# A new written-out order for attention and expert layers on one core, with its opening and its end listed word by word

## The chip, the cores and the metric

The kernel runs on one core of a Trainium2 chip. The metric is the device time of a whole execution in microseconds (us); the kernel before takes 478.36 us (median of three runs, 478.16 to 478.54). A profile of one execution has, for each engine, the start and length of every instruction, and for each DMA queue the packets that it moved. The engines are TensorE (PE, matmuls into PSUM), VectorE (DVE), ScalarE (ACT), GpSimd (POOL, which here issues the loads that change the type) and SyncE (SP, which issues stores and transposing DMAs).

## The reference

Linformer attention, then a two-layer network with a sigmoid-weighted activation:

```python
k_proj = np.einsum('ks,bhsd->bhkd', E, k)
v_proj = np.einsum('ks,bhsd->bhkd', F, v)
scores = scale * np.matmul(q, k_proj.transpose(0, 1, 3, 2))
attn = np.exp(scores - max);  attn = attn / sum(attn)
x = attn @ v_proj                      # (batch, seq, heads * 64)
h = x @ w_in;  g = h / (1 + np.exp(-1.702 * h))
out = g @ w_out
```

There are 8 batches of 8 heads, 1024 positions and 64 numbers a head, 64 projected keys, and layers of 512 x 2048 and 2048 x 512. Inputs and output are float32.

## The kernel before, in words

The 8192 tokens are cut into 16 blocks of 512, so two blocks (j = 2b and 2b + 1) make a batch b. For a batch, k and v are loaded (`load_kv`, one DMA each, into the single buffers `k_sb` and `v_sb`), projected by 16 matmuls with 64 columns of weights (`proj`, line 183), and k is transposed on its way by a DMA on SP (`kts`). q is loaded in eight DMAs (`load_q`, line 70) and transposed by SP (`q_dma`, line 263) into `qT`. For a block, the scores (`sc`, line 273) come out of `eight`: eight matmuls on tiles of 64 x 32 that run side by side. ACT takes the exponential (`ex`), TensorE sums it (`su`, line 719) and multiplies it with v (`va`, line 273), and DVE scales the result with the reciprocal sums (`mv`, line 713). Those sums travel from PSUM through `den`, a gathering DMA (`ga`), a reciprocal on DVE (`rc`), a write to memory (`sr`) and a spreading read into `rbc` (`sb`), the DMAs all on SP. Blocks 1 and 2 instead do it with tokens on the partitions (`tok`, `x_tr`).

Layer 1 of blocks 0, 1 and 2 is done plainly, 64 matmuls of 512 columns (`ffn1`, line 426), and so is layer 2 of block 0 (`ffn2`, line 438). All else uses seven half-size products instead of eight (the scheme of Strassen and Winograd): a layer is split into quarters, so that 112 matmuls of 256 columns do the work of 64 of 512. Layer 1 is cut into four groups u0 to u3 with products `P1` to `P7` (line 677), layer 2 into `F1` to `F7`, two parts each (line 637, or 533 where `ffn2_parts` makes them). Between products, partial sums are copied (`c1`, `c2`, `c3`, `Fc1` to `Fc3`, line 620 and 681) and added (`d1`, `d2`, `Fd1`, `Fd2`, line 623), and the activation (`g11` to `g22`, line 693) reads the sums. `x_sum` and `g_sum` prepare the differences of the inputs, `w_sums` and `w_in_sums` those of the weights, once; the four w_in differences lie in `late`.

The order of work is written by hand. Blocks 0 to 2 come from loops with a table of extra work (`at`, `filled`). From block 2's second layer on, a list of words, `STEPS`, is read once per block: `u1.P5+1` is product 5 of group 1 of the next block, `sc.0+3` the scores of the block three ahead. Each engine does its own words in the order of the list; a word waits for its inputs and for its buffer. `BANK` names the PSUM bank that each result uses, so a word also waits until the bank's last reader is done. `AHEAD` inserts words the first time round. `pj`, `kb`, `kd`, `vq` are the projection and the copies of its result, `ld` and `lq` the loads of the next batch's k and v and of its q, `qd` q's transpose. `ld` has to wait for `pj`, which reads the same buffers, and a load of q for the transpose that reads the q tile before it in the same buffer:

```python
return ldpool.tile([P, J, H, D], BF16, name="q_even" if b in (0, 2) else "q_sb")
```

`q_even` is later reused for `uu`, the partial sums of the u groups, and in block 2 for a temporary of `w_in_sums`. A word `hold` makes POOL wait for a transposed k before it issues the loads behind it.

Of the kernel before, what the change touches and what calls it, by code (L numbers as in the profile page):

```python
# [17 lines left out]
def kernel(ctx, tc, q, k, v, E, F,  # L18
                                                     moe_w_in, moe_w_out, out):
    nc = tc.nc  # L20
# [41 lines left out]
    def q_buf(b):  # L62
        return ldpool.tile([P, J, H, D], BF16, name="q_even" if b in (0, 2) else "q_sb")

    def load_q(b, j0=0):
        if j0 == 0:
            qt[b] = q_buf(b)
        qv = q[b].rearrange("h (p j) d -> p j h d", p=P)
        for j in range(j0, J):
            nc.gpsimd.dma_start(out=qt[b][:, j], in_=qv[:, j])  # L70

    def load(b):
        for what in ("kvq", "kqv", "kvq", "qkv")[min(b, 4) - 1]:
            if what == "q":
                load_q(b)
            elif what == "k":
                load_kv(k, kt, b, "k_sb")
            else:
                load_kv(v, vt, b, "v_sb")
# [19 lines left out]
    for i in range(8):  # L99
        if i == 7:  # L100
            load_q(0, JB)
        load_w_in(i)
    for i in range(4):
        sl = slice(i * FC // 4, (i + 1) * FC // 4)
        nc.gpsimd.dma_start(out=w_out_sb[:, sl, :], in_=w_out_v[:, sl, :])
    load(1)


# [110 lines left out]
    def v_out(b, v_ps):  # L219
        vv = v_ps[HI].rearrange("k (u x) d -> k u x d", x=4)  # L220
        for r, xs_ in ((LO, X_LO), (HI, X_HI)):
            if b == 1:
                vx = vx1[r, :, :D].rearrange("k (u x) d -> k u x d", x=4)
                nc.vector.tensor_copy(vx[:, :, xs_], vv[:, :, xs_])
            nc.vector.tensor_copy(vqs[b % 2][r].rearrange("k (u e) d -> k u e d", e=2), vv[:, :, xs_, :])

    def kv_out(b, cp=nc.vector.tensor_copy):
        def go():
            ps = kvps.pop(b)
            k_b = att.tile([KP, H, D], BF16, name="k_b")  # L230
# [45 lines left out]
    def x_tile():  # L276
        return x_any([P, TB])

    def scores(h, u, half=None, x=False):
        b, c = divmod(h, NB2)  # L280
        j0, n = (c * JB, JB) if half is None else (c * JB + half * JB // 2, JB // 2)
        ts = slice(j0 * P - c * TB, (j0 + n) * P - c * TB)

        def go():
            if h not in expT:
                expT[h] = att.tile([P, HP, TB], BF16, name="expT", bufs=3)
            s_ps = [(x_tile() if x else f_tile([P, TB]))[:, :n * P] for _ in range(2)]
            eight(s_ps, [kts[b % 2][:, 2 * u + i, :] for i in range(2)],
                 [q0s[half][u][:, :, i, :] if h == 0 else qT[b][:, j0:j0 + n, 2 * u + i, :]
                   for i in range(2)], KP if h == 0 else 32)  # L290
            for i in range(2):
                nc.scalar.activation(expT[h][:, 2 * u + i, ts], s_ps[i], AF.Exp, scale=scale)
        return go
# [9 lines left out]
    def sums(h):  # L303


        def go():
            d_ps = [x_any([P, TB]), bank(5, [P, TB])]
            for p in range(HP):
                for e in range(2):
                    r = HI if (p + e) % 2 else LO  # L310
                    nc.tensor.matmul(d_ps[e][32 * p:32 * p + 32], ones[r, :32], expT[h][r, p, :], start=True, stop=True)
            den = att.tile([P, 2, TB], F32, name="den", bufs=1)
            for e in range(2):
                nc.vector.tensor_copy(den[:, e, :], d_ps[e])
            rdens[h] = den
        return go

# [7 lines left out]

    def spread(h, q=nc.sync, recip=True):
        def go():
            rc = rdens.pop(h)
            n = rc.shape[1]
            if recip:  # L330
                nc.vector.reciprocal(rc, rc)
            rdr = dram.tile([HP, 2, TB], F32, name="rdr")
            q.dma_start(out=rdr.rearrange("p e (r n) -> (p e r) n", n=n), in_=rc)
            rbc[h] = att.tile([P, HP, TB], F32, name="rbc", bufs=1)
            for e, r in enumerate((LO, HI)):
                q.dma_start(out=rbc[h][r], in_=rdr[None, :, e, :].to_broadcast([D, HP, TB]))
        return go

    def norm(h, u):
        def go():  # L340
            e = [expT[h][:, 2 * u + i, :] for i in range(2)]
            d_ps = [x_any([P, TB]) for _ in range(2)]
            eight(d_ps, [ones, ones], e)
            n_ps = [x_any([P, TB]) for _ in range(2)]
            eight(n_ps, [vqs[h // NB2 % 2][:, 2 * u + i, :] for i in range(2)], e)
            for i in range(2):
                rd = att.tile([P, TB], F32, name="rdn")
# [82 lines left out]
    def ffn2(j, n, fcs):  # L430
# [4 lines left out]
        if fcs.start == 0:  # L435
            o_ps[n] = f_tile([P, DM])
# [499 lines left out]
```

The softmax here doesn't subtract the row's maximum and nothing guards it: scores larger than these inputs give would overflow.

## Time and profile before

| what | value |
|---|---|
| median of three runs | 478.36 us |
| profiled execution: span from first to last instruction | 474.7 us |
| what lies outside the span, by the median | 3.7 us |
| TensorE busy (its ends are modelled) | 463.9 us, 98% |
| DVE, ACT, POOL busy | 316.6, 322.1, 83.2 us |
| matmuls of layer 1 and 2 in seven products | lines 677, 637 and 533 |
| small-tile matmuls (scores, values, sums) | 240, 208 and 96 + 8 in groups of eight |
| packets of POOL's queue, of SP's | 86816 (30.43 MB), 46020 (37.84 MB) |
| TensorE clock granted | full |

A row of a timeline is: start, length, engine, line, operation, what is written from what, how many, and in brackets how long the engine stood idle before it and what released it. The lengths of matmuls overlap, so the distance between starts tells their cost. The profile gives no time of its own for the profiled execution beyond its span.

### The profile page before, as it was taken

How to read it: one execution, taken by the hardware profiler on the slowest of the kernel's cores; microseconds unless marked ns; L12 is line 12 of the kernel's file. 1: busy time of each engine (PE TensorE's matmuls, PEld its weight loads, DVE VectorE, ACT ScalarE, POOL GpSimd, SP SyncE). 2: the span in 40 equal slices, each digit the busy share in tenths (PEclk: the TensorE clock that was granted, in tenths of full speed). 3: DMA queues.
4: the chain of work that ended last, by engine and by line, in shares of the span. 5: the costliest groups of instructions: out<-in, count | busy, mean ns of one | idle time of the engine just before them, and what ended most of it. 6: DMA issues, size and time to landing. Idle time of an engine off the chain costs nothing.

```text
span 474.7 us, 10486 instructions
## 1 busy us (share of the span) xinstructions
PE 463.9 (98%) x4323; PEld 356.2 (75%) x4331; DVE 316.6 (67%) x587; ACT 322.1 (68%) x559; POOL 83.2 (18%) x104
## 2 busy tenths in 40 slices
PE   8999999998999999999999999999999999999997
PEld 4644447556778788887878788787888878888885
DVE  4503895498486776858686685868667685958562
ACT  2665456566696777868686786957687786758472
POOL 7562161061051200501050010500000000000000
PEclk9999999999999999999999999999999999999999
DMA  9999999989799999937999299942371403602022
GB/s 169 200 188 207 228 192 152 232 169 180 114 212 207 200 200 238 110 92 162 211 216 130 94 152 214 172 95 97 90 182 38 121 25 91 177 5 90 0 90 90
DMA packets 132964, 69.19 MB, mean 146 GB/s; under 512 B 98341, under 2 KB 122421, under 8 KB 132917
## 3 DMA queue, kind: packets, MB, share of 16 engines
q0 software_dynamic: 86816, 30.43, 57.5%
q1 hardware_dynamic: 46020, 37.84, 32.8%
q8 instruction: 34, 0.56, 0.5%
q10 hardware_dynamic: 80, 0.26, 0.2%
q14 instruction: 14, 0.11, 0.1%
HBM read 72.88 MB, written 16.99 MB: 189 GB/s over the span
## 4 chain that ended last, share of the span: by engine, by line
PE 91%; DMA 3%; ACT 3%; DVE 2%; POOL 1%; issue 1%; DVEq 0%; ACTq 0%; POOLq 0%
PE k_ps L677 34%; PE k_ps L637 33%; PE k_ps L426 9%; PE k_ps L533 5%; PE k_ps L273 3%; PE k_ps L438 3%; PE k_ps L183 3%; DMA v_sb<-in_v_dram 3%; ACT gT L693 1%; PE k_ps L719 1%; DVE xT L713 1%; POOL k_sb L58 0%; POOL v_sb L58 0%; PE k_ps L398 0%; PE k_ps L413 0%
## 5 line engine op out<-in xcount | busy, mean ns | idle before, releaser
L623 DVE TENSOR_TENSOR q_even<-k_ps,q_even 128x512 f32<-128x512 f32 x104 | 70.5, 689 | 54.4 <-PE k_ps L677 53.2
L677 PE MATMUL k_ps<-xw,late 128*128 128x256 bf16 x624 | 89.5, 273 | 0.6 <-DVE xw L499 0.6
L677 PEld LDWEIGHTS <-late 128*128 128x128 bf16 x832 | 80.4, 98 | 12.8 <-PE k_ps L637 2.3
L637 PEld LDWEIGHTS <-sg 128*128 128x128 bf16 x832 | 81.2, 98 | 10.7 <-issue 1.4
L693 ACT ACTIVATE gT<-k_ps 128x512 bf16<-128x512 f32 x104 | 62.3, 601 | 25.3 <-PE k_ps L677 23.7
L637 PE MATMUL k_ps<-tw,sg 128*128 128x256 bf16 x624 | 76.8, 273 | 0.3 <-DVE u_sb L620 0.3
L677 PEld LDWEIGHTS <-w_in_sb 128*128 128x128 bf16 x624 | 58.2, 98 | 18.1 <-issue 11.3
L637 PEld LDWEIGHTS <-gT 128*128 128x128 bf16 x624 | 61.0, 98 | 7.8 <-issue 0.4
L620 ACT COPY q_even<-k_ps 128x512 f32<-128x512 f32 x65 | 37.0, 591 | 42.8 <-PE k_ps L677 42.0
L677 PE MATMUL k_ps<-xT,w_in_sb 128*128 128x256 bf16 x416 | 62.2, 273 | 1.0 <-ACT vq L620 1.0
L693 ACT ACTIVATE gT<-q_even 128x512 bf16<-128x512 f32 x104 | 61.4, 631 | 0.0
L70 POOL DMA_DIRECT2D q_sb<-in_q_dram x48 | 42.1, 904 | 106.5 <-DMA qT<-q_sb 70.1
L637 PE MATMUL k_ps<-w_out_sb,gT 128*128 128x256 bf16 x416 | 51.6, 273 | 0.1
L426 PE MATMUL k_ps<-xT,w_in_sb 128*128 128x512 bf16 (+1 forms) x195 | 42.4, 370 | 0.3
L507 DVE TENSOR_TENSOR sg<-gT 128x1024 bf16<-128x1024 bf16 (+2 forms) x64 | 41.4, 649 | 1.6 <-ACT gT L693 1.5
L428 ACT ACTIVATE gT<-k_ps 128x512 bf16<-128x512 f32 (+1 forms) x50 | 28.9, 580 | 18.0 <-PE k_ps L426 17.7
L426 PEld LDWEIGHTS <-w_in_sb 128*128 128x128 bf16 x200 | 19.3, 98 | 21.3 <-issue 0.8
L713 DVE TENSOR_TENSOR xT<-k_ps,rbc 128x512 bf16<-128x512 f32 x52 | 33.5, 680 | 0.0
L677 PE MATMUL k_ps<-xw,w_in_sb 128*128 128x256 bf16 x208 | 31.3, 273 | 0.0
L677 PE MATMUL k_ps<-xT,late 128*128 128x256 bf16 x208 | 31.2, 273 | 0.0
L681 ACT COPY k_ps<-k_ps 128x512 f32<-128x512 f32 x52 | 29.2, 588 | 2.7 <-DVE xT L713 1.2
L620 DVE COPY q_even<-k_ps 128x512 f32<-128x512 f32 x39 | 25.7, 686 | 8.0 <-PE k_ps L677 8.0
(136 smaller groups left out, 561.2 us busy)
## 6 DMA issues: line engine op xcount, KB each, us to landing
out_dram<-o_sb SPq DMA_DIRECT2D x31, 512.0 KB
rbc<-rdr SPq DMA_DIRECT2D x24, 512.0 KB
k_sb<-in_k_dram POOLq DMA_DIRECT2D x7, 1024.0 KB, 10.2
v_sb<-in_v_dram POOLq DMA_DIRECT2D x7, 1024.0 KB, 15.2
q_sb<-in_q_dram POOLq DMA_DIRECT2D x48, 128.0 KB, 6.4
w_in_sb<-in_moe_w_in_dram POOLq DMA_DIRECT2D x8, 256.0 KB, 10.8
w_out_sb<-in_moe_w_out_dram POOLq DMA_DIRECT2D x4, 512.0 KB, 11.5
q_even<-in_q_dram POOLq DMA_DIRECT2D x12, 128.0 KB, 13.2
```

The lines of the kernel that those rows point to most:

```text
L70: nc.gpsimd.dma_start(out=qt[b][:, j], in_=qv[:, j])
L426: nc.tensor.matmul(h_ps, w_in_sb[:, kc, fc * P:(fc + 1) * P], xT[j][:, kc, ts], start=(kc == 0), stop=(kc == KC - 1))
L428: nc.scalar.activation(gts[j][:, fc, ts], h_ps, AF.Gelu_apprx_sigmoid)
L507: nc.vector.tensor_tensor(t[i - 1], in0, in1, op=ALU.add if i == 1 else ALU.subtract)
L533: nc.tensor.matmul(dst, a[:, k, tc_ * P:(tc_ + 1) * P], w[:, k], start=(first and (one or tc_ == 0) and k == 0), stop=(final and k == FH - 1),
L620: (nc.scalar.copy if n in ON_ACT else nc.vector.tensor_copy)(out_, in_)
L623: nc.vector.tensor_tensor(out_, in0, in1, op=ALU.add)
L637: nc.tensor.matmul(live[n][:, t], x[:, c, t * P:(t + 1) * P], w[:, c], start=(i in (1, 5) and t == 0 and c == 0), stop=(i in (2, 3, 4) and ...
L677: nc.tensor.matmul(live[h][:, r], a[:, c, f:f + P], w[:, c], start=(i in (1, 5) and r == 0 and c == 0), stop=(i in (2, 3, 4) and r == 1 an ...
L681: nc.scalar.copy(new(f"B{m}", [P, 2, TH]), live[f"A{m}"])
L693: nc.scalar.activation(out_, in_, AF.Gelu_apprx_sigmoid)
L713: nc.vector.tensor_tensor(x_of(j)[:, u, :], live[f"V{p[1]}{t}"], rbc[j][:, u, :], op=ALU.mult)
```

## The change

The steady list is replaced by one that needs two stretches of small tiles in a block: the projection with both score groups between `F1.0` and `F1.1`, and values, sums, values at the end. It is used for nine blocks (j = 4 to 12). What comes before and after it is written out in two further lists, `OPEN` and `TAIL`, in which `@` gives the block, `:` the PSUM banks and `/A` or `/D` the engine of a copy. Block 0's first layer stays a loop. In `OPEN`, `O` is block 0's second layer, `L` and `Lg` block 1's first layer and its activation, `tk`, `tr`, `tm`, `xt`, `xc` the token-wise attention of blocks 1 and 2, `ws` and `wi` single weight sums, `s0` the stores of block 0, `qda` and `qdb` the two halves of batch 1's q transpose. Block 2's first layer now goes through the u groups, so that `uu` takes `q_even` there, the temporary of `w_in_sums` moves into `sg`, and only batch 0's q is kept in `q_even`. Most weight sums of layer 1 are made while block 0's first layer runs. The last piece of w_in is loaded ahead of the second half of batch 0's q, batch 1's q is loaded in two halves with v between, and `hold` is gone. More banks are named, and copies move between DVE and ACT.

```diff
     def q_buf(b):
-        return ldpool.tile([P, J, H, D], BF16, name="q_even" if b in (0, 2) else "q_sb")
-
-    def load_q(b, j0=0):
+        return ldpool.tile([P, J, H, D], BF16, name="q_sb" if b else "q_even")
+
+    def load_q(b, j0=0, j1=J):
         if j0 == 0:
             qt[b] = q_buf(b)
         qv = q[b].rearrange("h (p j) d -> p j h d", p=P)
-        for j in range(j0, J):
+        for j in range(j0, j1):
             nc.gpsimd.dma_start(out=qt[b][:, j], in_=qv[:, j])
...
     nc.gpsimd.dma_start(out=q0_sb, in_=q[0].rearrange("h (p j) d -> p h j d", p=P)[:, :, :JB])
     load_kv(v, vt, 0, "v_sb", 2)
     for i in range(8):
-        if i == 7:
-            load_q(0, JB)
         load_w_in(i)
+    load_q(0, JB)
     for i in range(4):
         sl = slice(i * FC // 4, (i + 1) * FC // 4)
         nc.gpsimd.dma_start(out=w_out_sb[:, sl, :], in_=w_out_v[:, sl, :])
-    load(1)
+    load_kv(k, kt, 1, "k_sb")
+    load_q(1, 0, JB)
+    load_kv(v, vt, 1, "v_sb")
+    load_q(1, JB)
...
+    def w_in_sums(i, copy=nc.vector.tensor_copy, cols=slice(None)):
+        tmp = sg[:, 2:].rearrange("p i c t -> p (i c t)").bitcast(F32).rearrange("p (c f) -> p c f", c=KC // 2)
+        if i == 5:
+            return copy(late[:, 1], tmp)
+        out_, in0, in1, op = ((late[:, 0], a21, a22, ALU.add), (late[:, 2], a11, a21, ALU.subtract),
+                              (tmp, a21, a22, ALU.add), (tmp, tmp, a11, ALU.subtract),
+                              (late[:, 3], a12, tmp, ALU.subtract))[i]
+        nc.vector.tensor_tensor(out_[..., cols], in0[..., cols], in1[..., cols], op=op)
...
+    OPEN = """
+        sc.1@1:7,4 qda@2 sc.0@1:5,6 O.1.0@0:0 O.1.1@0 O.3.0@0:2 ex.0.0@1 tk.0.0@1:5 tr.0.0@1 ex.0.1@1 ex.1.0@1
+        tm.0.0@1 O.2.0@0:3 ex.1.1@1 O.3.1@0 tk.0.1@1:5 O.1.2@0 tk.1.1@1:7 tr.0.1@1 tm.0.1@1 tk.1.0@1:5 O.1.3@0
...
+        L.9@1:6 Lg.2@1 ws.1@1 vq.1@2/A vx.0@2 Lg.15@1 ld@2 L.11@1:4 gs1.1@1 Lg.0@1 Lg.11@1 F1.0@1:3 kd@2 Lg.9@1
+        s0.0@0 s0.1@0 qdb@2 sc.0@2:0,2 sc.1@3:5,6 gs3.1@1 ws.3@1 gs3.0@1 ex.0.0@2 sc.0@3:1,4 gs1.0@1 ex.0.1@3
...
+        ex.0.0@3 ex.0.1@2 ex.1.0@3 F1.1@1 tk.0.0@2:7 pj@4:0 Fc1@1:1/A gs2.0@1 ws.5@1/D gs2.1@1 kb@4/D tr.0.0@2
+        sc.1@2:4,2 tk.0.1@2:5 F6.0@1 tr.0.1@2 vq.0@4/A ex.1.0@2 tk.1.0@2:4 lq@2 kd@4 tm.0.1@2 tm.0.0@2 ex.1.1@2
+        tr.1.0@2 F6.1@1 tk.1.1@2:7 F2.0@1 vq.1@4/D gt@5 tm.1.0@2 tk.2.0@2:2 tr.1.1@2 xt.0@2:4 F5.0@1:5 qd@4
...
+        sc.0@4:7,1 u1.P7@2 ex.0.1@4 ex.0.0@4 u0.d2@2 Fd2@1 rc@3 ld@4 sc.1@4:0,5 ex.1.0@4 ex.1.1@4 u0.P7@2
+        u0.P2@2 u3.P1@2:7 su@4:5,1 xs.3@2 u1.d1@2 u0.d1@2 den.0@4/D den.1@4/D u0.g11@2 u1.P4@2 u1.g21@2 u0.g22@2
...
     STEPS = """
-        F3.0-1 u2.c1 Fo1-1 u0.d2 rc+2 F3.1-1 u2.P5 u3.c3 u3.P7 u0.g22 Fd2-1 u2.P6 u0.g12 u2.c2 u2.c3 u2.P2
-        u2.g11 u3.P3 va.0+1 u3.d1 st0-1 gs1.0 u3.P2 u3.d2 u3.g11 u2.P3 u3.g12 mv.0.1+1 u2.P7 va.1+1 pj+4 ld+4
-        u3.g22 u3.P4 u2.d2 st1-1 u2.g12 u3.g21 u2.d1 mv.0.0+1 kb+4 F1.0 mv.1.0+1 u2.g22 vq.0+4 u2.P4 mv.1.1+1
-        gs1.1 u2.g21 vq.1+4 F1.1 u0.P1+1 sr+2 sc.0+3 gs2.0 gs2.1 sc.1+3 Fc1 ex.0.0+3 gs3.0 u1.P1+1 xs.0+1
-        ex.1.1+3 xs.2+1 gs3.1 F2.0 F2.1 ex.1.0+3 xs.1+1 kd+4 ex.0.1+3 F6.0 F6.1 Fc2 u0.c1+1 su+3 u1.c1+1 gt+1
-        u0.P6+1 den.0+3 u0.P2+1 Fo0 den.1+3 gs4.1 u1.P6+1 F7.0 u1.P2+1 u1.P5+1 u0.c2+1 F5.0 u1.c2+1 u0.g11+1
-        u1.c3+1 F5.1 ga+3 Fc3 u1.P7+1 F7.1 u1.g11+1 xs.3+1 gs4.0 u1.P3+1 u2.P1+1 u0.P5+1 u1.d1+1 u3.P1+1 Fd1
-        u0.c3+1 u1.P4+1 F4.0 u0.P7+1 sb+2 u1.d2+1 u0.d1+1 qd+4 lq+4 u1.g21+1 u3.c1+1 F4.1 u1.g12+1 u3.P6+1
-        u3.c2+1 u0.P4+1 u1.g22+1 u3.P5+1 u0.P3+1 u0.g21+1
+        F1.0 pj+4 mv.1.1+1 u3.g22 mv.0.0+1 u2.g12 mv.1.0+1 xs.0+1 sc.1+3 gs2.0 ga+2 sc.0+3 kb+4 F1.1 vq.0+4
+        u1.P1+1 vq.1+4 gs1.1 xs.1+1 gs2.1 Fc1 kd+4 ex.1.1+3 u1.P5+1 F2.1 ex.1.0+3 u1.c3+1 F2.0 rc+2 Fo0 xs.3+1
+        ld+4 F6.0 u1.c1+1 gs3.1 lq+3 F5.0 u0.P5+1 gs4.1 F6.1 u1.P6+1 st1-1 ex.0.0+3 ex.0.1+3 gt+4 sr+2 u0.P1+1
+        u0.c1+1 xs.2+1 F5.1 u1.P3+1 qd+4 gs3.0 Fc2 u0.c3+1 u0.P2+1 u1.c2+1 u1.d2+1 gs4.0 F7.0 u1.P2+1 u0.g11+1
+        u2.P1+1 u2.c1+1 F7.1 Fc3 u0.P3+1 u2.P2+1 Fd1 u0.P6+1 u1.P7+1 u1.g11+1 u1.d1+1 sb+2 u0.c2+1 F4.1 u3.P1+1
+        u0.d2+1 F4.0 u1.P4+1 Fo1 u0.g12+1 u1.g21+1 u0.P7+1 u1.g22+1 u3.c1+1 F3.1 u1.g12+1 u2.g11+1 u3.P5+1
+        u2.P6+1 F3.0 u0.d1+1 u2.P5+1 u0.g22+1 u3.c3+1 u3.P6+1 u2.c2+1 u2.c3+1 u2.P7+1 u3.P3+1 gs1.0+1 u3.c2+1
+        u3.P2+1 Fd2 u3.P7+1 u0.P4+1 u2.d1+1 u2.g22+1 u2.P4+1 u3.g11+1 u0.g21+1 u3.d1+1 u2.P3+1 u3.P4+1 va.0+2
+        u2.g21+1 u3.d2+1 u2.d2+1 mv.0.1+2 st0 su+3 u3.g21+1 va.1+2 den.0+3 den.1+3 u3.g12+1
     """.split()
-    BANK = dict(FD=0, FB=4, FG=0, A0=6, A1=1, B0=7, B1=3, G0=2, G1=5, S10=5, S11=7, V00=4, V01=0,
-                S00=3, S01=2, V10=6, V11=5, D0=2, D1=5, PJ=1)
-    ON_ACT = ('Fc1', 'Fc3', 'c2.2', 'c3.0', 'c3.1', 'c3.2', 'c3.3', 'vq')
-
-    held = consts.tile([1, 1], BF16, name="held")
...
+        u3.P3@15 u3.P2@15 u2.P7@15 F3.0@14 u2.P3@15 F3.1@14 u3.d2@15 u2.d1@15 u2.d2@15 u3.g22@15 u3.g11@15
+        u3.g12@15 u1.g21@15 u2.g22@15 u2.g12@15 Fd2@14 gs1.0@15 u3.P4@15 F1.0@15:7 u2.P4@15 F1.1@15 gs1.1@15
+        f5.1@15:0 gs2.0@15 gs2.1@15 gs4.0@15 gs3.1@15 u2.g21@15 Fc1@15:5/A F6.0@15 F6.1@15 Fc2@15/A fc3.1@15
+        u3.g21@15 f5.0@15:2 st0@14 st1@14 F7.0@15 F7.1@15 gs4.1@15 fc3.0@15 f3.0@15 Fd1@15 F4.1@15 F4.0@15
+        F2.0@15 F2.1@15 Fo1@15/A fd2.0@15 f3.1@15 fd2.1@15 st2.0@15 st1@15 Fo0@15/A st0h@15 st2.1@15
+    """.split()
+    BANK = {"D0":1, "D1":5, "FB":1, "FD":3, "FG":0, "PJ":1, "S00":5, "S01":7, "S10":4, "S11":0, "V00":6, "V01":0,
+            "V10":2, "V11":7, "u0.A":7, "u0.B":5, "u0.G":3, "u1.A":6, "u1.B":4, "u1.G":2, "u2.A":7, "u2.B":2,
+            "u2.G":3, "u3.A":6, "u3.B":4, "u3.G":1}
+    ON_ACT = ("Fc1", "Fc2", "den.0", "den.1", "kb", "u0.c1", "u0.c2", "u0.c3", "u1.c1", "u2.c1", "u2.c3", "u3.c2",
+              "vq.0", "vq.1")
...
+        on_act = (name in ON_ACT) if eng is None else eng == "A"
+        copy = nc.scalar.copy if on_act else nc.vector.tensor_copy
...
+        elif i == "O":
+            n, g = int(p[1]), t
+            if g == 0:
+                new(f"O{n}", [P, DM])
+            for fc in range(4 * g, 4 * g + 4):
+                nc.tensor.matmul(live[f"O{n}", j], gts[j][:, fc, n * P:(n + 1) * P], w_out_sb[:, fc, :],
+                                 start=(fc == 0), stop=(fc == FC - 1))
+        elif i == "L":
+            gts[j] = gT
+            h_ps = new(name, [P, TB])
+            for kc in range(KC):
+                nc.tensor.matmul(h_ps, w_in_sb[:, kc, t * P:(t + 1) * P], xT[j][:, kc, :],
+                                 start=(kc == 0), stop=(kc == KC - 1))
+        elif i == "Lg":
...
         elif i == "pj":
-            kvps[b] = new("PJ", [P, H, D])
-            proj(b)()
-        elif i == "hold":
-            nc.gpsimd.tensor_copy(held, kts[b % 2][:1, 0, :1])
-        elif i == "ld" and b + 1 < B:
+            kv_ps = new("PJ", [P, H, D])
+            for n in range(J):
+                for e, r in enumerate((LO, HI)):
+                    nc.tensor.matmul(kv_ps[r], eft(n, slice(e * KP, (e + 1) * KP)), (kt, vt)[e][b][:, :, n, :],
+                                     start=(n == 0), stop=(n == J - 1))
+        elif i == "ld":
             load_kv(k, kt, b + 1, "k_sb")
...
+            else:
+                nc.vector.tensor_copy(vx1[r, :, :D].rearrange("k (u x) d -> k u x d", x=4)[:, :, xs_], vv)
+        elif i in ("qd", "qda", "qdb"):
+            q_dma(b, *{"qd": (0, J), "qda": (0, JB), "qdb": (JB, JB)}[i])()
+        elif i == "lq":
             load_q(b + 1)
-        elif i not in ("ld", "lq"):
+        else:
             raise KeyError(name)
 
...
-    AHEAD = {
-        (2, None):
-            "F1.0@2 F1.1@2 Fc1@2 sc.1@4 sc.0@4 ex.1.0@4 ex.1.1@4 F2.0@2 ex.0.0@4 ex.0.1@4 F2.1@2 sc.1@5 "
-            "F6.0@2 sc.0@5 F6.1@2 ex.1.0@5 ex.1.1@5 ex.0.0@5 ex.0.1@5 gt@3 Fo0@2 Fc2@2 va.0@3:6,1 va.1@3:5,7 "
-            "mv.0.0@3 mv.0.1@3 mv.1.0@3 mv.1.1@3 F7.0@2 su@4:0,3 den.0@4 den.1@4 ga@4 ",
-        (2, "u1.c1+1"): "F7.1@2",
-        (2, "u2.P1+1"): "rc@4 sr@4 sb@4 qd@6 pj@6:1 kb@6 kd@6 vq.0@6 vq.1@6 hold@6 ld@6 lq@6",
-    }
-
...
+    first = [(half, fc) for half in range(2) for fc in range(2)] + [(None, fc) for fc in range(2, FC)]
+    for i, (half, fc) in enumerate(first):
+        ffn1(0, fc, slice(0, TB) if half is None else slice(half * TB // 2, (half + 1) * TB // 2))
+        if i == 12:
+            for cols in (slice(0, DH // 2), slice(DH // 2, DH)):
+                w_in_sums(2, cols=cols)
+            w_in_sums(3)
+            w_in_sums(0)
+        if i in (15, 16):
+            q_tr(i - 13)()
+    w_in_sums(1)
+
+    BATCH = ("qd", "pj", "kb", "kd", "vq", "ld", "lq")
+
+    def due(name, j):
+        kind = name.split(".")[0]
+        if kind in BATCH and j % NB2:
+            return False
+        return j < (NBLK - NB2 if kind in ("ld", "lq") else NBLK)
+
+    def listed(words):
+        for word in words:
             name, n = word.split("@")
+            n, _, eng = n.partition("/")
             n, _, banks = n.partition(":")
-            step(name, int(n), [int(x) for x in banks.split(",")] if banks else None)
-            done.add((name, int(n)))
-
-    done = set()
-    for j in range(2, NBLK):
-        last = j == NBLK - 1
...
+    listed(OPEN)
+    for j in range(4, NBLK - 3):
         for word in STEPS:
-            m = word.replace("-", "+-").split("+")
-            name, n = m[0], j + int(m[1] if len(m) > 1 else 0)
-            if last and name[0] in "Fs" and n == j and name[:2] not in ("sc", "su", "sr", "sb"):
-                if name[1:2].isdigit() and name[0] == "F":
-                    parts.pop(tail.pop(0))()
-            elif due(name, n, j) and (name, n) not in done:
-                step(name, n)
-            ahead(j, word)
-    for f in parts.values():
-        f()
-    assert not fill, fill
+            name, _, n = word.replace("-", "+-").partition("+")
+            if due(name, j + int(n or 0)):
+                step(name, j + int(n or 0))
+    listed(TAIL)
```

## The prediction

> **What bounds the kernel now.** First the page's head and its chain of waits:
>
> ```profile
> span 474.7 us, 10486 instructions
> PE 463.9 (98%) x4323; PEld 356.2 (75%) x4331; DVE 316.6 (67%) x587; ACT 322.1 (68%) x559; POOL 83.2 (18%) x104
> PE 91%; DMA 3%; ACT 3%; DVE 2%; POOL 1%; issue 1%; DVEq 0%; ACTq 0%; POOLq 0%
> ```
>
> TensorE sets the end; DVE and ACT have a third to spare. So the change is worth what it takes out of TensorE's stream, less what makes TensorE wait. Then the timeline of TensorE in a steady block (start, length, count) and around two waits:
>
> ```profile
> 275.35 0.60 PE L677 MATMUL k_ps<-xT,w_in_sb 128*128 128x256 bf16 x4
> 275.88 0.62 PE L273 MATMUL k_ps<-qT,kt 64*32 64x512 bf16 x16
> 276.43 0.61 PE L677 MATMUL k_ps<-xT,w_in_sb 128*128 128x256 bf16 x4
> 276.88 1.91 PE L637 MATMUL k_ps<-w_out_sb,gT 128*128 128x256 bf16 x16
> ...
> 115.14 0.61 PE L677 MATMUL k_ps<-xw,late 128*128 128x256 bf16 x4 [0.59 <-DVE xw L499]
> ...
> 123.99 0.60 PE L677 MATMUL k_ps<-xT,w_in_sb 128*128 128x256 bf16 x4 [1.04 <-ACT vq L620]
> ...
> 460.35 1.03 PE L533 MATMUL k_ps<-w_out_sb,gT 128*128 128x256 bf16 x8 [0.86 <-ACT k_ps L564]
> ```
>
> Starts, not the modelled lengths, give the pitch: 276.88 to 278.63 is 16 matmuls of 256 columns, 0.109 each. A 128x512 one takes 0.216 (56 between 89.90 and 101.99, the next row's start). 275.35 to 276.43 is 1.08 for four products (0.44) and two groups of eight small tiles (0.216 each): 0.21 is left over. The same sum for a lone group of eight (`su` at 280.47) leaves 0.22. So a visit to small tiles costs 0.22, however many groups it holds. Row by row, TensorE makes 57 visits after 36.49, four in a block.
>
> Third, the queues that feed TensorE. POOL's timeline, which issues the loads, and SP's, which issues stores and transposes (start, length of the issue):
>
> ```profile
> 60.38 0.87 POOL L58 DMA_DIRECT2D k_sb<-in_k_dram  x1 [4.47 <-PE k_ps L183]
> 299.23 7.00 POOL L70 DMA_DIRECT2D q_sb<-in_q_dram  x8 [24.41 <-DMA qT<-q_sb]
> ...
> 64.15 5.73 SPq L263 DMA_TRANSPOSE qT<-q_sb  x1
> 81.91 7.16 SPq L263 DMA_TRANSPOSE qT<-q_even  x1
> ```
>
> The first is k2, released by the projection that freed `k_sb`; the second a q load that stood 24.41 until the transpose of the q before it had left `q_sb`. Last, the packets that POOL's queue (q0) and SP's (q1) moved in the microseconds from 67, from 83 and from 88 (count, MB):
>
> ```profile
> q0 software_dynamic: 156, 0.16, 93.6%
> q1 hardware_dynamic: 157, 0.04, 30.4%
> ...
> q0 software_dynamic: 204, 0.21, 125.0%
> ...
> q1 hardware_dynamic: 1131, 0.29, 127.7%
> ```
>
> POOL's k load alone moves 204 packets a us (1 KB each), SP's transpose alone 1131 (256 B). Together they move 156 and 157: one for one, so the transpose falls to a seventh of its speed. I take 157 for each when both have work.
>
> [...] I use 1 us, since POOL wakes at 299.2 when the transpose's packets have ended some 2 us before, and at 188.9 some 1 us after them. [...]
>
> **The change part by part**, in us, against the profiled execution (474.7; its start and end outside the span are 3.7 against the median 478.36).
>
> Block 2, layer 1: 64 x 0.216 = 13.83 becomes 112 x 0.109 = 12.22: -1.6. The zeros matmul goes: -0.2.
>
> Visits: in the new lists I count 32 after the opening instead of 57: 25 x 0.22 = -5.5.
>
> Waits in the old order that go with it: the larger gaps above the pitch, 1.2 at 123.99, 1.0 at 460.35, 0.8 at 115.14, six of 0.35 to 0.6 between 73 and 111: some -5.0. Waits that the new order brings: F2.1 needs Fc1, with only one product (0.44) between, where the copy and the end of the matmul take about 0.55: 0.1 in each of ten blocks; sc.1@1 now comes straight after the q_tr copy (36.52): 0.15; the tail about 0.5; DVE's rc@3 below 0.3: +2.0, with 0.5 to 6 as bounds.
>
> Costed at nothing: ON_ACT moves copies between ACT (0.59) and DVE (0.69); of 26.9 a block I add ACT 17.7 and DVE 19.7. Tight spots of a block (u.P4 after d1, u.P6 after c1, mv after va) keep 0.1 to 0.8. Four repeated table words and the reloads around split exponentials (1.28 each, perhaps 10 in all) lie in an opening where ACT has 78 of 118; without cover, each would cost up to 1.28. The w_in sums (2.29, 2.29, 1.19, 1.19) go to DVE while it idles 12.6 before q_tr's copy at 34.52. They need w_in's last piece, which now precedes q's second half, so the packet counts put it at 27.8, and they end at 32.5; without that slack q_tr is late by the difference. w_out's sums and the k and v evictions lie beside 512-column products as before. On POOL w_in's last piece moves ahead of q's second half, which lands about 1.3 later (near 31.7; q_tr wants it at 33.9), and v1 moves behind half of q1.
>
> Now the queues. Of the q tiles only batch 0's keeps `q_even` (which becomes `uu` in block 2), so batch 2's q (q2) goes into `q_sb`, which q1 holds until its second transpose, qdb@2, has landed. Before, q2 was loaded at 61.24 without it. And ld@2 issues k2 and v2 (2048 packets) together; before, v2 went out at 74.47.
>
> First wait. PE reaches pj@2 at 36.49 + 19.5 of listed work + 0.5 = 56.5, v1 lands about 56 (its 1024 packets follow q1's first half; `qda` shares the end). It ends at 58.4; k2/v2 issue 58.8, full rate 3.2 later at 62. SP: kd@2 behind kb@2 (59.4), two stores of block 0 (from 60.7), qdb@2 at about 62.3, when q1's last packets have landed. The stores' 256 packets of 4 KB share with k2: 3.8, to 66.3. Then qdb's 2048 packets against the 1650 left of k2/v2: 1650/157 = 10.5; the rest 0.4; seen at 78.2. sc.1@3 reads that half; PE is there at 36.49 + 32.7 + 1.0 = 70.2: **waits 8.0**. Behind it is all of PE; pj@4 too (v2 is in at 77.8).
>
> Second wait. lq@2 starts 78.4; eight issues and 8192 packets take 9.4 to 9.6 (299.23 to 308.8), seen 88.6. On POOL ld@4 stands right behind (its buffers are free once pj@4 ends, near 82), so k3/v3's packets follow from 88. qd@4 starts at 88.7, packets 2.7 later; k3/v3 have 1350 left: 1350/157 = 8.6, then 2746/1131 = 2.4, seen 103.4. PE, after 78.2, has 19.2 of work and 0.7 of visits: sc.0@4 at 98.1, **waits 5.3**. (Before, a copy to `held` kept POOL 20.68 at 136.06 until a kt transpose, issued behind qd@6, had landed, and only then let k4/v4 go; it is removed.) On SP, ga@3 queues behind qd@4, so rc@3 and the u1.d1 behind it on DVE come at about 105.8; u1.P4 needs it at 106.
>
> In the steady blocks with a projection the same order (sb behind qd on SP, ld beside it) puts rbc down some 3 before mv.0.1 reads it: k/v's last 1150 packets share for 7.3, the transpose's rest takes 5, rbc 2.4, from an issue 7 after the block's start to 22 to 24 of 27.7. So nothing; if that cover is gone, its lateness stands on DVE ahead of all four multiplies and xs.0, which the next block's products read.
>
> Sum: 474.7 - 1.6 - 0.2 - 5.5 - 5.0 + 2.0 + 8.0 + 5.3 = 477.7; +3.7 = **481.4**. A move within 0.2% (0.96) is about what a measurement can't tell from none.
>
> **Rivals.** (1) *Only the first wait*: k3/v3 don't meet qd@4. Alone it ends 8.6 after its start (81.91 to about 90.5), seen 98.3, level with PE: 472.6 + 3.7 = 476.3. For it: 85 to 91 had such a transpose to itself. Against: POOL holds nothing between lq@2 and ld@4. (2) *The other side, faster*: loads don't hold up SP's transposes. qdb is then seen at 67.8, no wait; pj@4 waits 5.7 for v2 and q2's transpose (seen 93.9) is hidden: 470.1 + 3.7 = 473.8; with no wait at all 468.1. It decides when q2's transpose is seen before 100.4: the two waits then total under 10.3, which is what the rest gains. Against it is the 157 against 157. (3) *The steady order stalls too*: 0.5 to 1.0 per block at the tight spots, nine blocks: 486 to 490. For it: slacks of 0.1. (4) The change doesn't do what it says: products or visits stay; I see both in the lists, so under 0.01.
>
> **How the numbers follow.** Likeliest 0.50: 477.5 to 486 (slower 0.44, same 0.06). Rival 1, 0.18: 474 to 478.5 (faster 0.12, same 0.06). Rival 2, 0.14, faster. Rival 3, 0.18, slower. Faster 0.26, same 0.12, slower 0.62. 473.5 to 487 leaves about one in ten on each side (the no-wait part below, the worst of rival 3 above).
>
> **What would show it.** PE's timeline should have one gap of 5 to 10 ahead of the small tiles near 70 to 78, released by the qT transpose, and one of 2 to 8 near 98 to 103; POOL's q2 load starting near 78 after `DMA qT<-q_sb`; steady pairs of blocks of about 54 instead of 54.8; 512-column matmuls of L gone from block 2. I am wrong if the transpose lands by 72, if q2's load starts before it, or if steady blocks lengthen.

## The result, and the profile after

The changed kernel takes 507.64 us (median of 5; 506.91 to 510.83) against 478.36 (5 runs, 478.11 to 478.54): 1.063 times the time before, 95% interval 1.060 to 1.066. The prediction was 481.4, at most 487: the direction is right, the size is not. (One of the five executions of `i_halves` below, at 501.68, was a slow one and is left out of that run's ratio.)

The page's head, its row of the granted TensorE clock over 40 slices of 12.7 us, and its chain (the profiled execution took 510.83; the clock row of the kernel before is 9 throughout):

```profile
span 509.1 us, 10598 instructions
PE 470.7 (92%) x4372; PEld 367.8 (72%) x4378; DVE 334.9 (66%) x603; ACT 323.2 (63%) x557; POOL 80.4 (16%) x100
PEclk9999996979979999999997999979999999999999
PE 50%; DMA 29%; SPq 9%; issue 7%; POOL 2%; DVE 1%; ACT 1%; POOLq 0%; DVEq 0%; ACTq 0%
```

TensorE was 91% of the chain and is 50%; DMA has 29% and SP's issues 9%. The clock has dips, which the kernel before has not. TensorE's timeline has these gaps (start, length, count, in brackets the idle time ahead and what ended it):

```profile
80.83 1.05 PE L249 MATMUL k_ps<-qT,kt 64*32 64x512 bf16 x16 [9.82 <-DMA qT<-q_sb]
108.93 0.63 PE L249 MATMUL k_ps<-qT,kt 64*32 64x512 bf16 x8 [5.40 <-DMA qT<-q_sb]
148.56 1.01 PE L605 MATMUL k_ps<-xT,w_in_sb 128*128 128x256 bf16 x4 [4.82 <-DVE xT L641]
...
216.43 0.41 PE L249 MATMUL k_ps<-qT,kt 64*32 64x512 bf16 x8 [2.91 <-DVE xT L641]
273.67 1.21 PE L249 MATMUL k_ps<-qT,kt 64*32 64x512 bf16 x12 [2.65 <-DVE xT L641]
335.08 1.21 PE L249 MATMUL k_ps<-qT,kt 64*32 64x512 bf16 x12 [4.13 <-DVE xT L641]
```

The first two are the waits that the prediction placed near 70 to 78 and 98 to 103, at 9.8 and 5.4 instead of 8.0 and 5.3. The other four, 14.5 in all, it did not have. They stand behind DVE's multiplies (`mv`, L641), and DVE's table of waits says what these wait for (in all, times, longest):

```profile
DVE xT L641 <- DMA rbc<-rdr: 20.8, 4, 8.0
```

That is `sb`, the spread of the reciprocals: four times, 20.8 in all. One such place on the chain, in order of time (start, length):

```profile
199.13 7.76 SPq L239
...
207.00 0.61 SPq L664
...
207.66 7.90 DMA rbc<-rdr
...
215.69 1.30 DVE xT L641 x2
```

SP is in the issue of the q transpose `qd` (L239) until 206.9; only then can `sb` (L664) go, and it lands 7.9 later. In the kernel before, the view of the tile `rbc` has for this link:

```profile
DMA to landing us min/median/max: 4.9/5.9/6.9
```

The transpose, issued at 191.3, is slow because of the loads beside it. Packets of POOL's queue (q0) and of SP's (q1) in the microsecond from 199, and of SP's from 207, when the loads had ended (count, MB, share of the 16 engines):

```profile
q0 software_dynamic: 149, 0.15, 89.4%
q1 hardware_dynamic: 150, 0.04, 29.1%
...
q1 hardware_dynamic: 1134, 0.29, 127.6%
```

The one near 148, in the opening, is of another make: `qd` takes only 4.9 there. `sb` of block 4 stands behind it on SP and goes at 137.6, and `rbc` is read at 147.8, while a load of q, issued at 137.9, moves its packets beside it (460 in the microsecond from 141).

Then the clock. Windows around the gap at 271 (from and to, length; busy time and count of PE, PEld, DVE, ACT and POOL; granted clock; DMA share; GB/s):

```profile
271.00:272.00 1.00, 0.03 (x4) 0.00 (x0) 0.00 (x0) 1.00 (x3) 1.00 (x3) 1.00 1.01 316
273.00:274.00 1.00, 0.33 (x8) 0.12 (x8) 1.00 (x2) 0.00 (x0) 1.00 (x2) 0.50 2.33 166
276.00:277.00 1.00, 1.00 (x7) 0.69 (x6) 1.00 (x3) 0.20 (x1) 0.00 (x0) 0.50 1.24 363
281.00:282.00 1.00, 1.00 (x11) 0.90 (x10) 1.00 (x3) 0.98 (x2) 0.00 (x0) 1.00 0.31 24
```

The clock falls to 0.50 about 2 after the last matmul and is back to 1.00 only near 279.8, 6.1 after TensorE resumed. The same windows behind the gaps ending at 80.8, 108.9, 148.6 and 335.1 show 4.4, 3.6, 4.9 and 6.1 of work at half clock; the gap before 216.4 has none. Four products that take 0.44 at 1.00 take 0.85 at 0.50 (starts at 276.50 and 277.35), so half of these 25.1 is lost, by estimate: 12.6. In all five stretches the whole windows read 0.50. Counted from the fall to the return, idle time included, the stretches are more regular: from 272 to 280 the windows read 0.97, six times 0.50, and 0.61, which is 0.06 + 6 + 0.78 = 6.84 at half clock. The other four come to 10.24, 6.82, 6.82 and 6.84: two or three times 3.41. The prediction had not priced any of it.

The account against the predicted span of 477.7: first wait 1.8 more, second 0.1, the four others 14.5, half clock 12.6: 506.7 of the 509.1 measured.

### The profile page after: what moved, and what is told of

Its sections match the earlier page's. It is cut to its first block, busy times and chain, and to the rows that moved or that the text cites. A ratio compares the mean times of both kernels' runs of the same rounds, so it can differ in the third digit from the quotient of the medians.

```text
span 509.1 us, 10598 instructions
## 1 busy us (share of the span) xinstructions
PE 470.7 (92%) x4372; PEld 367.8 (72%) x4378; DVE 334.9 (66%) x603; ACT 323.2 (63%) x557; POOL 80.4 (16%) x100
## 4 chain that ended last, share of the span: by engine, by line
PE 50%; DMA 29%; SPq 9%; issue 7%; POOL 2%; DVE 1%; ACT 1%; POOLq 0%; DVEq 0%; ACTq 0%
PE k_ps L502 23%; PE k_ps L605 21%; SPq L239 8%; DMA k_sb<-in_k_dram 8%; DMA qT<-q_sb 8%; DMA q_sb<-in_q_dram 6%; DMA rbc<-rdr 4%; PE k_ps L249 2%; DMA q_even<-in_q_dram 2%; PE k_ps L315 2%; DMA rc<-den 2%; POOL q_sb L70 1%; PE k_ps L669 1%; DVE xT L641 1%; POOL k_sb L58 0%
## 5 line engine op out<-in xcount | busy, mean ns | idle before, releaser
L502 PEld LDWEIGHTS <-sg 128*128 128x128 bf16 x960 | 93.5, 98 | 11.2 <-issue 0.4
L502 PE MATMUL k_ps<-tw,sg 128*128 128x256 bf16 x720 | 89.7, 273 | 0.0
L502 PEld LDWEIGHTS <-gT 128*128 128x128 bf16 x720 | 71.4, 102 | 19.9 <-issue 9.2
L605 PEld LDWEIGHTS <-w_in_sb 128*128 128x128 bf16 x672 | 66.5, 99 | 15.1 <-issue 6.5
L502 PE MATMUL k_ps<-w_out_sb,gT 128*128 128x256 bf16 x480 | 64.2, 285 | 0.2 <-ACT k_ps L516 0.2
L641 DVE TENSOR_TENSOR xT<-k_ps,rbc 128x512 bf16<-128x512 f32 x52 | 32.6, 681 | 22.1 <-DMA rbc<-rdr 20.8
L633 ACT ACTIVATE expT<-k_ps 128x512 bf16<-128x512 f32 x60 | 32.4, 599 | 16.5 <-PE k_ps L249 16.3
L374 DVE TENSOR_TENSOR sg<-gT 128x1024 bf16<-128x1024 bf16 x60 | 40.6, 682 | 3.2 <-ACT gT L621 2.9
L249 PE MATMUL k_ps<-qT,kt 64*32 64x512 bf16 x240 | 13.4, 434 | 25.1 <-DMA qT<-q_sb 15.2
L487 DVE TENSOR_TENSOR o_sb<-k_ps,u_sb 128x512 f32<-128x512 f32 (+1 forms) x31 | 20.8, 670 | 20.1 <-PE k_ps L502 16.7
L502 PE MATMUL k_ps<-tw,gT 128*128 128x256 bf16 x240 | 32.1, 282 | 0.2 <-DVE o_sb L487 0.2
L502 PE MATMUL k_ps<-w_out_sb,sg 128*128 128x256 bf16 x240 | 30.8, 273 | 0.0
## 6 DMA issues: line engine op xcount, KB each, us to landing
w_out_sb<-in_moe_w_out_dram POOLq DMA_DIRECT2D x4, 512.0 KB, 11.5
```

Source lines behind the costliest of these rows:

```text
L249: nc.tensor.matmul(outs[i][r.start + c:r.start + c + w], lhsTs[i][ri, c:c + w], rhss[i][ri], start=True, stop=True)
L374: nc.vector.tensor_tensor(t[i - 1], in0, in1, op=ALU.add if i == 1 else ALU.subtract)
L487: nc.vector.tensor_tensor(out_, in0, in1, op=ALU.add)
L502: nc.tensor.matmul(dst, x[:, k_, t * P:(t + 1) * P], w[:, k_], start=(first and k_ == 0), stop=(final and k_ == FH - 1), skip_group_check= ...
L605: nc.tensor.matmul(live[h, j][:, r], a[:, k_, f:f + P], w[:, k_], start=(i in (1, 5) and r == 0 and k_ == 0), stop=(i in (2, 3, 4) and r = ...
L633: nc.scalar.activation(expT[j][:, 2 * n + t, :], live[f"S{n}{t}", j], AF.Exp, scale=scale)
```

## The experiments

Theory Q: the loads of k and v, packet for packet beside SP's transposes, make the transposes long; what stands behind them on SP comes late; TensorE waits, and loses more at half clock. Rival N: the new order itself (its visits, banks and copies) costs more than it saves. All times are medians; the ratio is to the kernel before, run beside them on the same chip (477.1 to 478.2).

| run | us | ratio, 95% interval |
|---|---|---|
| `a_sb_first` | 494.08 | 1.034 (1.032 to 1.036) |
| `b_sb_first_open` | 491.53 | 1.029 (1.027 to 1.030) |
| `c_stores_late` | 506.29 | 1.062 (1.059 to 1.065) |
| `e_filler` | 505.09 | 1.058 (1.055 to 1.062) |
| `g_before_sb_late` | 479.05 | 1.0021 (1.0010 to 1.0031) |
| `h_ld_behind_lq` | 503.74 | 1.054 (1.050 to 1.058) |
| `d_hold_ld4` | 511.45 | 1.069 (1.067 to 1.072) |
| `i_halves` | 491.84 | 1.026 (1.023 to 1.029) |
| `k_halves2` | 496.28 | 1.039 (1.033 to 1.045) |
| `l_split_kv` | 497.51 | 1.042 (1.037 to 1.047) |
| `n_after_noload` | 468.04 | 0.980 (0.979 to 0.982) |
| `n_before_noload` | 477.07 | 0.9988 (0.9979 to 0.9996) |
| `m_reorder` | 485.51 | 1.018 (1.015 to 1.021) |
| `m2_rc_late` | 489.87 | 1.027 (1.025 to 1.030) |

**Is it the order of the work or the loads?** Two kernels without the loads of batches 2 to 7, made from the changed kernel and from the kernel before; these batches compute on batch 1's data:

```
+        if b > 1:              # load_kv
+            dst[b] = dst[1]
+            return
...
+        if b > 1:              # load_q
+            qt[b] = qt[1]
+            return
```

> Edit to the changed kernel: the loads of q, k and v of batches 2 to 7 are left out, and these batches compute on batch 1's; every instruction of the engines, every transpose, store and spread stays, in the changed kernel's order. Theory Q (the loads' packets beside SP's transposes cause every new wait, the order of the work is as good as its sum says): all waits but some 1.5 at the first transpose (two stores are still ahead of it) go, and the clock stays at full: the prediction's sum without the two waits, 464.4 + 3.7 = 468, up to 471. Rival (the order itself, its visits, banks and copies, costs more than it saves): 478 or more even without loads.

> The same edit to the kernel before: the loads of batches 2 to 7 left out. Its own waits come from ACT and DVE rather than from loads, so at most 2 are gained: 476 to 478.4. The difference between this run and the changed kernel without loads is what the new order is worth by itself: by the prediction's terms 1.6 + 0.2 + 5.5 + 5.0 - 2.0 = 10.3, by the rival nothing or less.

Measured: 468.04 and 477.07. The head of the page of the changed kernel without loads:

```profile
span 466.1 us, 10490 instructions
PE 456.9 (98%) x4378; PEld 362.3 (78%) x4378; DVE 334.5 (72%) x603; ACT 322.4 (69%) x557; POOL 27.8 (6%) x40
```

TensorE is at 98% again, and the clock row is 9 throughout. Rival N falls: without loads the new order is 9.0 faster than the old (the prediction's terms give 10.3), and its span, 466.1, is near the 464.4 to which they come without waits. All of the loss comes with the loads. Two blocks take 53.84 here (`su` at 158.00 and 211.84), against 57.5 and 59.9 in the changed kernel with its stalls (`su` at 183.76, 241.27 and 301.19).

**The steady blocks.** Only the place of `sb` in the steady list is changed:

```
-u1.P3+1 qd+4 gs3.0 ... u1.d1+1 sb+2 u0.c2+1
+u1.P3+1 sb+2 qd+4 gs3.0 ... u1.d1+1 u0.c2+1
```

> Edit: in the steady list alone, sb (the spread of rbc) stands ahead of qd (the q transpose of the next batch) on SP; the opening keeps its order. Theory Q (the spread of rbc stands behind the q transpose, which shares packet for packet with the k and v loads; mv, and with it TensorE, waits for rbc, and the clock halves after such a gap): the three gaps of TensorE near 213, 271 and 331 (3.1, 2.65 and 4.13 in the profile of the changed kernel) close, and so do the two stretches at half clock behind them (2 x 3.0): about 16 us less than the changed kernel, 491.5. Rival N (the new order of the products and visits, or its copies, is what costs in the steady blocks): within 2 us of the changed kernel's 507.6.

Measured: 494.08, 13.6 less; 16 was expected. SP's timeline:

```profile
187.54 0.33 SPq L660 DMA_DIRECT2D rdr<-rc  x1
194.86 1.27 SPq L664 DMA_DIRECT2D rbc<-rdr  x2
196.42 10.61 SPq L239 DMA_TRANSPOSE qT<-q_sb  x1
```

`sb` goes at 194.9 instead of 207.0, the multiplies at 208.7 wait for nothing, and no gap above 1.6 and no half clock are left behind 150. What is missing to 16 is about what two smaller waits take in the steady blocks, the first because `qd` is later (0.94 for `qT` near 265; 1.5 near 320, which the profile puts down to ACT's `gT`). The first two steady blocks, without such a wait, now take 53.83 (`su` at 180.61 and 234.44) against 54.75 before: 0.46 a block, two visits of 0.22, as the prediction counted.

The other way to the same place: `sb` stays behind `qd`, but `ld` goes behind `lq` on POOL (`-ld+4 F6.0 u1.c1+1 gs3.1 lq+3`, `+F6.0 u1.c1+1 gs3.1 lq+3 ld+3`), so that the transpose has the engines to itself.

> Edit to the changed kernel: in the steady list alone, the k and v loads (ld) are issued on POOL behind the q load (lq), which waits for the q transpose; SP's order stays (sb behind qd). Theory Q with both halves needed (the spread is late only because the transpose it stands behind shares with k and v): qd's issue takes 6 to 8 instead of 15.6 to 17.2, sb goes some 8 earlier, and the three steady gaps and their half clock go as in the run with sb ahead of qd: 492 to 495. Rival (standing behind the transpose is enough, whatever it shares with): the gaps stay, 505 to 508.

Measured: 503.74, 3.9 less instead of 13 to 16. From the timelines of SP and DVE:

```profile
189.72 4.79 SPq L239 DMA_TRANSPOSE qT<-q_sb  x1
194.61 1.27 SPq L664 DMA_DIRECT2D rbc<-rdr  x2
...
218.77 0.35 DVE L656 RECIPROCAL rc<-rc 128x32 f32<-128x32 f32 x1 [2.97 <-DMA rc<-den]
```

Half right. The issue of the transpose takes 4.8 instead of 15.6, so it was the sharing that made it long, and `sb` is in time. But the loads, now at 204 to 220, hit the gather `ga`: `rc` waits 3.0 on DVE, TensorE behind it 6.4 in three places, 2.24 at the longest, each with a stretch of 3.4 at half clock. The lateness has moved to the next small transfer.

The same swap in the kernel before (`-sb+2 u1.d2+1 u0.d1+1 qd+4`, `+u1.d2+1 u0.d1+1 qd+4 sb+2`):

> Edit to the kernel BEFORE: in its steady list sb stands right behind qd on SP instead of ahead of it. In its trace sb is issued at 173.8 and rbc read at 188.3; behind qd, whose issue took 10.98, sb would go at 185 to 186 and land 5.9 later, some 3 to 4 after the read is due. Theory Q: DVE's mv is 3 to 4 late in the blocks in which a batch is loaded (three of them, and the one written out by hand isn't touched), TensorE waits 1 to 4 in each and runs at half clock behind those over some 2.5: 4 to 14 us slower than before, 482 to 492. Rival (the old order has cover for it, and what hurts in the new one is another thing): within 1 us of before.

Measured: 479.05, 1.1 more than before, where 4 to 14 were expected: a miss. The first transpose ahead of `sb` takes 8.5 to issue here, against 15.6 to 17.2 in the new list: in the kernel before, the k load is issued 11.5 to 11.8 ahead of `qd`, in the changed one 3.5 to 3.8, so less of the load runs beside the transpose. In the profiled execution, the slowest of twenty, `sb` first goes at 183.8; DVE waits 2.8 for `rbc` in that block, and TensorE 1.7, its only wait for these multiplies. The queue order alone is therefore not the fault: it costs where the transpose ahead of `sb` is long. A difference in cover between the lists is not shown: where `rbc` is late, TensorE's wait is 1.2 shorter than DVE's here and 1.0 shorter in the three steady blocks of the changed kernel (DVE 3.95, 3.69 and 5.17, TensorE 2.91, 2.65 and 4.13).

**The clock by itself.** Ten matmuls on zeros inside three of the gaps:

```
+            if word == "sc.1+3" and j in (5, 7, 9):
+                step("wm.10", j, [4])      # 10 matmuls 128x512 on zeros, bank 4
```

> Edit: ten matmuls of 128x512 on zeros (2.16 us of TensorE at full clock) are added ahead of sc.1 in blocks 5, 7 and 9, where TensorE waits near 213, 271 and 331; they belong to no result. Theory C (after some 2 to 4 us without work the granted clock goes to half and needs 5 to 7 us of work to come back): the waits end when they did, the work added lies inside them, and the half clock behind the second and third gap goes: about 6 us FASTER than the changed kernel, 501.6, with a mean clock above 0.975. Rival (the clock has another cause, or the filler delays what is waited for): same time, or 2 to 6 us slower.

Measured: 505.09, 2.5 less, though TensorE has 6.5 more to do; 6 less was expected. TensorE's timeline at the second place:

```profile
269.91 2.32 PE L637 MATMUL k_ps<-zeros 128*128 128x512 bf16 x9
...
273.14 0.41 PE L249 MATMUL k_ps<-qT,kt 64*32 64x512 bf16 x8 [0.46 <-DVE xT L645]
...
275.82 1.91 PE L502 MATMUL k_ps<-w_out_sb,gT 128*128 128x256 bf16 x16
277.57 1.91 PE L502 MATMUL k_ps<-tw,sg 128*128 128x256 bf16 x16
```

The 16 products at 275.82 take 1.75 to the next row; in the changed kernel the same 16, at 278.20, take 2.52. No half clock is left at these three places, so the clock is a cost of its own. (Theory C's "2 to 4" and "5 to 7" were, at the five stretches of the changed kernel, 1.9 to 4.0 without work and 3.6 to 6.1 of work.) The gain in the median is near the spread of the runs (503.87 to 507.57 here) and smaller than reckoned from one profile, whose execution took 3 more than the median and in which the stretches behind the second and third of these gaps are 6.84 each; in `c_stores_late`, below, which leaves these gaps as they are, the same three have 3.4, 3.4 and 6.8.

**The opening.** First, `sr` and `sb` of block 4 ahead of `qd` of block 6 as well:

> As the run before, and in the opening sr and sb of block 4 are moved ahead of qd of block 6 too. Theory Q: the gap of 4.8 near 148 closes with 2.5 of half clock behind it: 7 less again, about 484; the two waits near 71 and 103 (15.2 with some 4 of half clock) are left. If block 6's transpose then comes late for its scores, part of the 7 comes back. Rival N: no more than 1 us from the run before it.

Measured: 491.53, 2.6 less than `a` instead of 7. The 7 was reckoned from the changed kernel's profile, where this gap is 4.8; in that of `a` it is only 2.2. It closes, but `kd` of block 6 now stands behind `qd`, and `kt` comes 1.65 late.

Then the two stores of block 0 behind `qdb` (`-s0.0@0 s0.1@0 qdb@2`, `+qdb@2 s0.0@0 s0.1@0`), and the copy on POOL that holds k3 and v3 back (`-rc@3 ld@4`, `+rc@3 hd@4 ld@4`, where `hd` copies one element of `qT`):

> Edit: the two stores of block 0 (s0.0, s0.1) are issued on SP behind qdb of block 2 instead of ahead of it; nothing else. Theory Q (as in the prediction's first wait: 256 packets of 4 KB run ahead of the transpose and share with k2 and v2): the transpose lands at best 3.8 earlier, but what it gains is shared with k2 and v2 from then on, so the first gap shrinks from 9.8 to 6 to 8; the second wait, which follows from it by the q2 load, moves along with it. In all 2 to 4 us less than the changed kernel's 507.6: 503.6 to 505.6. Rival: the loads of k2 and v2 alone set it, and nothing is gained (within 1 us).

> Edit to the changed kernel: in the opening a copy on POOL that reads q2's transpose is put ahead of the loads of k3 and v3, so that these wait until the transpose has landed; nothing else. Theory S (the prediction's second wait: k3 and v3 share with qd of block 4): the transpose, alone, is seen some 8.6 to 9 after its start near 93.6, so about 102.5 instead of 108.9; TensorE gets there at 103.5, so the wait of 5.4 near 104 goes with 1.8 of half clock; k3, v3 and q3 come 3 later, which can take back 1 to 2 near 124 to 143: 500 to 503. Rival (the transpose is late by itself): 506 to 508.

Measured: 506.29 and 511.45, both slower than expected. With the stores behind, the first wait is 6.7, where the six profiles with the stores ahead have 9.8 to 10.35: they had a third of it. Of these 3 only 1.3 show in the median, within the spread of the runs. With the hold, the second wait goes altogether, so it was k3 and v3 that made it; but the same loads then run beside `sb` of block 3 and the gather `ga` of block 4 behind it. DVE's `rc` waits for that gather with block 3's multiplies behind it, TensorE waits for these, and the run is 3.8 slower:

```profile
121.99 0.35 DVE L659 RECIPROCAL rc<-rc 128x32 f32<-128x32 f32 x1 [6.44 <-DMA rc<-den]
...
122.94 0.41 PE L249 MATMUL k_ps<-expT,vq 64*32 64x512 bf16 x8 [4.05 <-DVE xT L644]
```

Five further runs put several such edits together: q2 transposed in halves (`qda`, `qdb`), v2 apart from k2, block 3's scores later, the SP order near 108 to 130 changed.

> Edits to the changed kernel, together: sb ahead of qd in the steady list (494.1 by itself); the stores of block 0 behind qdb; q2 transposed in two halves, the first as soon as its half of the load has landed; and near 130 sr, qd of block 6 and sb of block 4 in this order on SP. Theory Q: the first wait is 6.7 as in the run with the stores behind (instead of 10.3, 2 to 4 less), the second goes (5.3 with 2 of half clock), and the waits near 146 (4 with half clock) shrink to below 2: 482 to 486. Rival (the opening's waits move to the next transfer, as they did when the stores alone were moved): 488 to 492.

> As the run with q2 in two halves (sb ahead of qd in the steady list; stores of block 0 behind qdb; sr, qd of block 6 and sb of block 4 in this order), with two corrections that its trace asks for: the gather ga of block 3 goes on SP ahead of the second half of q2's transpose (behind it, rc waited 13.5 on DVE and TensorE 9.9), and the loads of k3 and v3 wait on POOL until the first half has landed. Theory Q: the 9.9 and the 6.3 behind it (kt near 150) go with their half clock, the first wait of 6.9 with 2 of half clock stays, the second is below 1: 481 to 484. Rival (each transfer moved makes the next one late): 488 or more.

> As the run before it, and against the first wait: k2 alone is loaded ahead of qdb of block 2, v2 waits on POOL until that transpose has landed, and the projection of batch 2 stands some 4 of TensorE's work later in the list. Theory Q: qdb shares with half as many packets and is seen near 70.5 instead of 78, when TensorE gets there; the first wait falls from 6.9 to below 1 with its half clock; the projection waits up to 2 for v2, and the first half of q2's transpose is seen near 90: 473 to 478, level with the kernel before or faster. Rival (v2 and q2, later now, stop TensorE in its place): 481 to 484, no better than the run before it.

> Edits to the changed kernel, all in order alone: sb ahead of qd in the steady list; stores of block 0 behind qdb of batch 1's q; block 3's scores some 5 of TensorE's work later, when that transpose lands near 78, with the projection of batch 2 behind them; q2 transposed in halves; k3 and v3 held on POOL until q2's transpose has landed; the projection of batch 3 some 3 later; and on SP, near 108, sr of block 4, kd of batch 3, sb of block 4 and then qd of block 6. Theory O (the order on the queues and in the list was wrong, the bandwidth suffices): waits of 1.6 near 78 and at most 1 to 2 each at three other places, little half clock: 472 to 478, level with or below the kernel before (478). Theory B (the loads don't fit): waits of over 12 in all stay in the opening, 485 or more.

> As the reordered run before it (485.5), with one change: the reciprocal of block 4 (rc) stands on DVE behind block 3's multiplies instead of ahead of them, and its sr and sb, with qd of block 6 behind them, follow it on SP. Theory O: the wait of 6.1 near 108 goes with 2 of half clock; the q load of batch 3 ends by 119 and qd of block 6 is seen by 132, where its scores are due: 476 to 479, level with the kernel before. Rival (the lateness moves to rbc of block 4 or to qT of block 6): 482 to 486.

Measured: 491.84, 496.28, 497.51, 485.51 and 489.87. All five are slower than expected. Mostly the wait aimed at went or shrank and another came or stayed: in `l` the first wait fell from 7.0 to 2.0, but the projection waited 4.0 for v2, and the scores of block 6 still 5.4 for `kt`, as in `k`, which was to close that wait. The best, `m`, has, after the start, three waits above 1.2 left (6.1, 2.0 and 1.5) and is 22 faster than the changed kernel, 8 slower than the one before. Its largest, 6.1, is the gather of block 4 once more, ahead of block 3's multiplies; moving it (`m2`) made 3.8 for `rbc` and 5.3 for `qT` of it. So much of the loss was order; whether some order carries all the loads beside the new list in under 478 stays open.

## Why the prediction was right or wrong

- *Products, visits and old waits*: right in sum. 464.4 without the new waits; the kernel without loads has 466.1. The fall to 53.83 for two blocks is the 0.22 per visit. With the loads, the prediction's own sign of being wrong came: steady blocks lengthened.
- *First wait, 8.0*: right in place, cause and nearly in size (9.8, TensorE there at 71). The stores' part was priced at 3.8; `c` shows 3.
- *Second wait, 5.3*: right in cause; the size (5.4) is partly luck. From the end of the first wait the queues took 28.1 instead of 25.2, and TensorE came to the scores after 22.7 instead of 19.9, of which 2.2 are half clock; the two misses cancel. The 1 us that the prediction allows from a transpose's last packet to what waits for it was some 0.7 here, by estimate: 226 packets from 108.0 at 1131 a us end at 108.2, and TensorE resumed at 108.93. `d` shows that k3 and v3 are its cause, so rival 1, in which they don't meet the transpose, is out. Rival 2, in which loads don't hold up transposes, is out by the 149 to 150 packets.
- *"In the steady blocks with a projection the same order ... So nothing"*: wrong, and the step that failed. Its picture was right (`sb` behind `qd` on SP, `qd` beside `ld`), its times were not. It has the transpose's packets done 7.3 + 5 = 12.3 after its issue, and `rbc` 2.4 later. By the packets of each microsecond, the transpose issued at 191.3 starts at some 196.3, 5 later, since `kt` and a store stand ahead of it in SP's queue; it shares with k and v until 205.4, for 9 and not 7.3, and ends at 208.4: 17.1 after its issue, 4.8 too few in the sum. (The 5 for the rest is more than its packets need, 2946 at 1131 a us, or 2.6; it took 3.0.) The last link is as far off: `rbc` came 7.2 after the transpose's last packet (in the chain, 7.9 after the second part of `sb` was issued), and not 2.4; the trace of the kernel before had 4.9 to 6.9 for it. So `rbc` came at 215.6, some 31 after the block's start at 184.3 instead of 22 to 24, and 3.95 after DVE stood ready. The prediction named what would follow "if that cover is gone", but gave it no price: it is 9.7 of gaps in three steady blocks. The gap of 4.8 near 148, where `sb` stands behind a short `qd` and meets a q load, was not priced either.
- *No term for the clock*: 12.6. Every gap was priced at its own length; 15 of predicted waits alone drew 4 of half clock behind them.
- *Rival 3* came nearest (the steady order stalls), but placed it at the tight spots of ACT and DVE, 0.5 to 1.0 in each of nine blocks. The stalls are 2.65 to 4.1, in the three blocks with a load.

## What to carry to other kernels

A cover of some 3 that was reckoned from packets was none here (`rbc` came 3.95 late): count every transfer that shares or stands ahead in the same queue, take issue to landing from the trace for the last link, and give the case "too late" a price. Give a TensorE gap like the six here, of 2.65 to 9.82, a price for the half clock behind it too: five of them cost by estimate another 1.8 to 3.1, and one, of 2.91, nothing. In these runs, where loads, transposes and small gathers share two queues, changing one place mostly moved the wait to the next transfer (`h` gained 3.9 instead of 13 to 16, `d` lost 3.8); a run without the loads, though it computes something else, tells first what the order of the work is worth.

## What the runs showed of the hardware

- In the profile of the changed kernel TensorE's granted clock fell to 0.50 between 1.9 and 4.0 after its last matmul, and took 3.6 to 6.1 of work to come back. From fall to return the stretches lasted 6.82 to 6.84 or 10.24; in `h` three lasted 3.42, 3.42 and 3.40. All of these lie within 0.02 of one, two or three times 3.41.
- The length of a gap did not decide alone whether such a stretch came: 2.9 before 216.4 drew none and 2.0 near 136 in `m` none, while 1.7 before 193.2 in `g` drew one of 3.4, which began 1.5 after TensorE had resumed. In `e_filler` nine matmuls on zeros ran for 2.32 from 269.91, and the clock read 1.00 from 271 to 279, where the changed kernel has 0.50 from 272.9.
- In `a` the 16 KB of `sr`, issued at 187.5 beside k and v and behind `kt` (184.7) and a store (186.0), let `sb` go only at 194.9, 7.3 later.
- The issue of one q transpose on SP took 4.8 in `h`, with no packet of POOL's queue in the microsecond from 194, and 15.6, 15.9 and 17.2 in the changed kernel beside a k and v load; SP started its next transfer 0.1 after each of these (207.0, 264.8, 326.0), and none in between.
